# q and k laid out by the host: PE transposes out of a decay attention kernel with a gated projection behind it

## Chip, core and metric

The kernel runs on one core of a Trainium2 chip. The metric is device time in microseconds for one launch; what the host does to the inputs before the launch is not in it. The engines are named as in the profile: PE (TensorE, matrix products), with PEld for its weight loads, DVE (VectorE), ACT (ScalarE), POOL (GpSimd) and SP (SyncE, which issues most DMAs).

## What is computed

Causal attention with a per-position decay for 8 batches of 8 heads (sequence 576, head dimension 64), and on its output a gate from a causal convolution of 5 taps, a 512 x 512 projection, and a second projection.

```python
def _attn_ref(q, k, v, f):
    scores = scale * np.matmul(q, k.transpose(0, 1, 3, 2))
    cum = np.cumsum(np.log(np.clip(f, 0.0001, 1.0)), axis=-1)
    decay = cum[:, :, :, None] - cum[:, :, None, :]
    scores = np.where(causal, -1000000000.0, scores + decay)
    attn = np.exp(scores - np.max(scores, axis=-1, keepdims=True))
    attn = attn / (np.sum(attn, axis=-1, keepdims=True) + 1e-09)
    return np.matmul(attn, v)

def _moe_ref(x, w_val, conv_w, w_out):      # x: heads side by side, (8, 576, 512)
    for k in range(K):                      # K = 5, xp: x padded by 4 in front
        gate_pre += conv_w[k][None, None, :] * xp[:, k:k + S, :]
    gate = 1.0 / (1.0 + np.exp(-gate_pre))
    return gate * (x @ w_val) @ w_out
```

## The kernel before

**Pairs.** Two heads make a pair, and 32 pairs are worked through one after the other; four of them make a batch. A pair's 576 positions are four blocks of 128 rows and a tail of 64. Every product that feeds PE in its fast mode is split into a high part (rounded to the fast type) and a low part (the rest), so that three fast products replace one exact one: for q and k these are the tiles Xh and Xl, for the attention output xh and xl, for the gated value hh and hl. The first four pairs (i < NF) use exact products instead, from one unsplit tile Xf.

**Stages of a pair**, each written by a function of its own:

- `load_pair` (L401) loads q and k of the pair with positions on the partitions: two DMAs of q, two of k, and three small ones for the last 64 rows of both, into qn, kn and zn. `load_rest` (L415) loads the decay rows (dm, dl) and v, three DMAs for v, and masks dm on POOL (L434) and dl (L437).
- `plan_t` (L508) turns q and k on PE, so that the head dimension lies on the partitions: four transposes of q, four of k (L530), two of zn (L537). The result lies in PSUM. For i < NF it is copied to Xf; later DVE or ACT casts it to Xh, and DVE takes the difference to PSUM as Xl (L521).
- `plan_s` (L544) makes the scores, adds the decay and finds the row minimum on DVE (L604), takes the exponential on ACT (L608), and the normalisation (L380, L382) on POOL, DVE or ACT.
- `plan_pt` (L636) turns the probabilities on PE (L649, L667) and copies them out of PSUM into pt; `plan_pv` (L682) multiplies by v, copies the result to x, splits it into xh and xl (L718 on POOL) and makes the gate's convolution: for the first four pairs on PE, with diagonal matrices, later as five passes on DVE (L747; the first tap through L380 or L382).
- After the fourth pair of a batch `plan_moe` (L754) takes the sigmoid on ACT, multiplies by w_val on PE, gates and splits on DVE, ACT and POOL, and multiplies by w_out.

The weights arrive in a packed form and are decoded on ACT and DVE (`plan_w`, `decode`), conv_w too (`plan_cw`), which is also turned on PE (L871).

**What sets the order.** No instruction is issued where it is written. Each is handed to a planner (`Plan.add`, `Plan.dma`) with the engines that may run it, a duration for each, and a priority. `Plan.order` then goes through a modelled time and takes at each step the instruction that can start first, by priority among those that can start together, and so fixes one engine and one place on it for everything. Two tables steer it: OFF moves the priority of a class of instructions, PEN burdens a class on one of its engines, both by stage of the program. PORT names the classes of DVE instructions that the planner keeps apart from POOL's, and STICK how much PE prefers its present array mode. SP's queue and the engines are in order: what stands first is waited for.

Of the kernel before, what the change touches and what calls it, by code (L numbers as in the profile page):

```python
# [32 lines left out]
XZ, XK4, XK, XW = 512, 640, 704, 1216  # L33

# [9 lines left out]
OFF = {  # L44
# [21 lines left out]
}  # L66
PEN = {
# [5 lines left out]
    ("conv", "ACT"): (0.0, 0.0, 2.52, 7.5, 4.7, 2.58), ("conv", "DVE"): (0.0, 0.0, 0.38, 0.0, 0.0, 0.5),  # L73
    ("conv", "POOL"): (0.0, 0.0, 65.48, 22.89, 42.2, 42.68), ("cut0", "DVE"): (12.46, 0.0, 0.0, 0.0, 0.0, 0.0),
    ("diag", "DVE"): (0.33, 1.54, 0.91, 0.0, 0.0, 0.0), ("diag", "POOL"): (11.96, 28.56, 14.33, 0.0, 0.0, 0.0),
    ("hh", "ACT"): (0.0, 0.0, 0.06, 0.0, 0.0, 7.62), ("hh", "DVE"): (0.0, 0.0, 0.22, 12.6, 5.06, 1.54),
    ("hl", "DVE"): (0.0, 0.0, 9.17, 0.64, 3.65, 0.0), ("hl", "POOL"): (0.0, 0.0, 0.51, 0.54, 0.04, 22.01),
    ("load", "ACT"): (7.36, 0.0, 0.0, 0.0, 0.0, 0.0), ("load", "SP"): (0.03, 0.0, 0.0, 0.0, 0.0, 0.0),
    ("norm", "ACT"): (0.0, 0.04, 0.67, 0.05, 0.79, 15.64), ("norm", "DVE"): (0.77, 5.49, 22.53, 0.36, 6.39, 2.21),
    ("norm", "POOL"): (3.05, 17.25, 0.28, 44.42, 0.8, 0.08), ("sel", "DVE"): (29.3, 28.29, 53.65, 8.66, 76.26, 0.31),  # L80
    ("sel", "POOL"): (1.34, 0.0, 0.11, 0.0, 0.0, 9.64), ("start", "ACT"): (5.02, 0.0, 0.0, 0.0, 0.0, 0.0),
    ("start", "DVE"): (5.62, 0.0, 0.0, 0.0, 0.0, 0.0), ("start", "POOL"): (0.21, 0.0, 0.0, 0.0, 0.0, 0.0),
# [197 lines left out]
def tile_decay_attention_gated_mlp(  # L280
    ctx: ExitStack,
    tc: tile.TileContext,
    q: bass.AP,
    k: bass.AP,
# [8 lines left out]
    B, H = q.shape[0], q.shape[1]  # L293
# [3 lines left out]
    KC = conv_w.shape[0]  # L297
# [103 lines left out]
    def load_pair(i):  # L401
        b, h0 = divmod(i, G)
        h0, r = 2 * h0, i % NQ
        p = i - (1.0 if i else 9.0)
        for nm, src, t in (("qn", q, qn[r]), ("kn", k, kn[r])):
            for h in range(2):
                load("load", 0.6, p, t[:, :, h], src[b, h0 + h, 0:L0].rearrange("(n p) d -> p n d", p=P), (), [(nm, r, h)], early=i == 0)
            if nm == "qn":
                for h in range(2):
                    load("load", 0.1, p, zn[r][D * h:D * h + D, 0, D * h:D * h + D], q[b, h0 + h, L0:], [("zn0", r)], [("zq", r, h)], early=i == 0)  # L410
            else:
                load("load", 0.15, p, zn[r][0:D, 1].rearrange("p (h d) -> p h d", h=2), k[b, h0:h0 + 2, L0:].rearrange("h p d -> p h d"),
                     [("zn0", r)], [("zk", r)], early=i == 0)

    def load_rest(i):  # L415
        b, h0 = divmod(i, G)
        h0, r = 2 * h0, i % NQ
# [34 lines left out]
    for r in range(NQ):  # L452
        dve("start", 0.2, z + r, lambda r=r: nc.vector.memset(zn[r], 0.0), (), [("zn0", r)])
# [54 lines left out]
    def plan_t(i):  # L508
        r = i % NQ
        p = float(i) if i else -8.0  # L510

        def evict(nm, key, lo, n, pr):
            if i < NF:
                any_("TF", ap(n), pr, lambda eng: copy(eng, Xf[:, lo:lo + n], bank(key)[:, 0:n]), [key, *kxf], [("Xf", nm)])
                return

            def hi(eng):
                copy(eng, Xh[r][:, lo:lo + n], bank(key)[:, 0:n])

            def low():  # L520
                nc.vector.tensor_tensor(out=Xl[r][:, lo:lo + n], in0=bank(key)[:, 0:n], in1=Xh[r][:, lo:lo + n].bitcast(F32),  # L521
                                        op=ALU.subtract)
            any_("TH", ap(n), pr, hi, [key], [("Xh", r, nm)])
            dve("TL", n / 960.0 + 0.08, pr, low, [key, ("Xh", r, nm)], [("Xl", r, nm)])
# [416 lines left out]
```

## Time and profile before

| | |
|---|---|
| runs | 590.12, 590.6 and, disturbed, 1100.04 us; median 590.6 |
| profiled execution | span 588.0 us from first to last instruction (its own run time is not listed; the runs' median stands 2.6 us above) |
| granted PE clock | 0.997 on average |
| DMA | 92.54 MB in 136222 packets, 118474 of all under 512 bytes |

How to read it: busy time and share for each engine come first, then the chain that ended last, followed backwards from the last instruction to what released each step. A group's row gives the line, the engine, the operation, the tiles (out<-in), the count, the busy time and the mean of one instruction in ns, and behind the second bar the idle time of the engine just before and who ended it. A timeline row gives start, length, engine and instruction. Two rows on the DMA side belong to the change:

```profile
q1 hardware_dynamic: 136222, 92.54, 57.2%
...
kn<-in_k_dram SPq DMA_DIRECT2D x64, 128.0 KB, 6.3
```

The first is the queue's packets, megabytes and share of the 16 DMA engines' time; the second is an issue group with its count, size and median time to landing.

### The profile page before, as it was taken

The page shows a single profiled execution, that of the slowest core. Times are in us where ns is not written, and L with a number is a line of the kernel's source. Part 1 is how long each engine was busy: PE and PEld are TensorE (multiplying, and loading weights), DVE is VectorE, ACT ScalarE, POOL GpSimd, SP SyncE. Part 2 cuts the span into 40 slices and gives each one's busy share as a digit, 9 for nine tenths or more (in the row PEclk, how much of TensorE's full clock was granted, in tenths as well). Part 3 has the DMA queues.
Part 4 walks back from the last instruction along what each step waited for, and adds up shares of the span by engine and source line. Part 5 has one row for each costly group of instructions (what it writes and reads, how often), then busy time and mean ns, then how long its engine had stood idle before and what let it go on. Part 6 is the DMA issues. An engine that isn't in the chain of part 4 may idle for free.

```text
span 588.0 us, 14152 instructions
## 1 busy us (share of the span) xinstructions
PE 566.3 (96%) x4773; PEld 493.8 (84%) x4773; DVE 449.9 (77%) x1200; ACT 460.9 (78%) x1252; POOL 251.6 (43%) x397
## 2 busy tenths in 40 slices
PE   6798989999999999999999999999999999999997
PEld 5576768888789988889888998989988998889995
DVE  5668969799987989779778888696767778775550
ACT  4979969999987698779898889987887786984201
POOL 5121257333322654553554654343664666371200
PEclk9999999999999999999999999999999999999999
DMA  5999787575754566385667666564666645210002
GB/s 136 258 223 262 167 232 220 155 180 158 232 134 137 147 186 192 116 236 145 174 160 194 173 178 178 166 179 124 171 200 171 169 131 163 81 47 19 37 37 89
DMA packets 136294, 93.44 MB, mean 159 GB/s; under 512 B 118474, under 2 KB 118494, under 8 KB 136222
## 3 DMA queue, kind: packets, MB, share of 16 engines
q1 hardware_dynamic: 136222, 92.54, 57.2%
q8 instruction: 38, 0.62, 0.5%
q14 instruction: 34, 0.28, 0.2%
HBM read 82.60 MB, written 9.91 MB: 157 GB/s over the span
## 4 chain that ended last, share of the span: by engine, by line
PE 70%; DVE 10%; ACT 7%; DMA 7%; issue 2%; SPq 2%; POOL 1%; DVEq 0%; POOLq 0%; ACTq 0%
PE banks L360 56%; PE banks L649 8%; DVE banks L604 4%; ACT P L608 3%; PE banks L530 3%; SPq L387 2%; DVE gate L747 2%; DMA vt<-in_v_dram 2%; PE banks L667 1%; DMA ot<-in_moe_w_out_dram 1%; ACT pt L375 1%; DMA dm<-decd 1%; DMA ot<-in_moe_w_val_dram 1%; DMA wu<-in_moe_w_val_dram 1%; DVE negm L604 1%
## 5 line engine op out<-in xcount | busy, mean ns | idle before, releaser
L608 ACT ACTIVATE P<-banks,negm 128x128 f32<-128x128 f32 (+3 forms) x256 | 132.9, 536 | 26.6 <-DVE negm L604 26.3
L604 DVE CUSTOM_DVE_ANT_0 banks<-banks,dm 128x128 f32<-128x128 f32 (+3 forms) x256 | 120.6, 515 | 30.3 <-PE banks L360 19.1
L375 ACT COPY pt<-banks 128x256 f32<-128x256 f32 (+2 forms) x320 | 115.9, 437 | 28.7 <-PE banks L649 24.2
L382 POOL TENSOR_SCALAR P<-P,rz 128x384 f32<-128x384 f32 (+3 forms) x134 | 79.7, 611 | 73.3 <-DVE rz L618 36.7
L360 PE MATMUL banks<-xh,wall 128*128 128x288 f32 x512 | 108.7, 299 | 1.5 <-ACT pt L375 1.4
L747 DVE SCALAR_TENSOR_TENSOR gate<-x,cw,gate 128x576 f32<-128x576 f32 x112 | 103.0, 920 | 1.8
L360 PE MATMUL banks<-pt,vt 128*64 128x128 f32 (+2 forms) x1408 | 97.0, 293 | 3.5 <-ACT pt L375 2.9
L360 PEld LDWEIGHTS banks<-pt,vt 128*64 128x64 f32 x1408 | 86.0, 138 | 15.6 <-ACT pt L375 4.3
L434 POOL TENSOR_SCALAR_AFFINE_SELECT dm<-dm 128x256 f32<-128x256 f32 x126 | 55.7, 467 | 96.6 <-DMA dm<-decd 90.2
L360 PE MATMUL banks<-wall,hh 128*128 128x512 f32 x288 | 93.0, 404 | 1.1 <-ACT P L608 0.9
L649 PE MATMUL banks<-ident,P 128*128 128x128 f32 x640 | 89.3, 277 | 4.0 <-ACT P L380 1.4
L360 PEld LDWEIGHTS banks<-xh,wall 128*128 128x128 f32 x512 | 83.5, 188 | 3.6 <-ACT pt L375 1.6
L649 PEld LDWEIGHTS banks<-ident,P 128*128 128x128 f32 x640 | 71.3, 140 | 12.2 <-ACT P L380 3.4
L360 PE MATMUL banks<-xl,wall 128*128 128x288 f32 x256 | 75.4, 295 | 0.0
L718 POOL TENSOR_TENSOR xl<-x,xh 128x576 fp32r<-128x576 f32 x32 | 50.6, 1583 | 48.9 <-ACT xh L375 48.9
L360 PEld LDWEIGHTS banks<-wall,hh 128*128 128x128 f32 x288 | 51.0, 188 | 11.7 <-ACT P L608 2.3
L360 PE MATMUL banks<-Xh 128*128 128x288 f32 (+4 forms) x280 | 58.4, 346 | 0.6 <-ACT P L608 0.5
L380 ACT ACTIVATE P<-P,rz 128x128 f32<-128x128 f32 (+3 forms) x114 | 58.2, 574 | 0.6 <-DVE rz L618 0.3
L360 PE MATMUL banks<-wall,hl 128*128 128x512 f32 x144 | 56.5, 392 | 0.0
L608 ACT ACTIVATION_READ_ACCUMULATOR P<-banks,negm 128x1 f32 x256 | 54.1, 211 | 0.0
L360 PE MATMUL banks<-Xh,Xl 128*128 128x288 f32 (+4 forms) x280 | 52.9, 314 | 0.0
L360 PE MATMUL banks<-Xl,Xh 128*128 128x288 f32 (+4 forms) x280 | 52.9, 313 | 0.0
(108 smaller groups left out, 933.3 us busy)
## 6 DMA issues: line engine op xcount, KB each, us to landing
dm<-decd SPq DMA_DIRECT2D x62, 640.0 KB, 5.9
out_dram<-ot SPq DMA_DIRECT2D x36, 256.0 KB, 2.3
dl<-decd SPq DMA_DIRECT2D x62, 144.0 KB, 3.7
qn<-in_q_dram SPq DMA_DIRECT2D x64, 128.0 KB, 2.8
kn<-in_k_dram SPq DMA_DIRECT2D x64, 128.0 KB, 6.3
vt<-in_v_dram SPq DMA_DIRECT2D x64, 128.0 KB, 3.1
zn<-in_q_dram SPq DMA_DIRECT2D x64, 16.0 KB, 3.1
zn<-in_k_dram SPq DMA_DIRECT2D x32, 32.0 KB, 2.8
```

Of the source, the lines that this page charges most:

```text
L360: nc.tensor.matmul(out, lhsT=lhsT, rhs=rhs, start=start, stop=stop)
L375: (eng.copy if eng is nc.scalar else eng.tensor_copy)(out=out, in_=in_)
L380: eng.activation(out=out, in_=in_, func=AF.Copy, scale=col)
L382: eng.tensor_scalar(out=out, in0=in_, scalar1=col, scalar2=0.0, op0=ALU.mult, op1=ALU.add)
L387: lambda e: (nc.sync if e == "SP" else nc.scalar).dma_start(out=out, in_=in_), reads, writes, **kw)
L434: nc.gpsimd.affine_select(out=t, in_=t, pattern=[[0, 2], [-1, P]], base=0, channel_multiplier=1, compare_op=ALU.is_ge, fill=-BIG)
L530: nc.tensor.transpose(out=bank(key)[:, n * P:(n + 1) * P], in_=src[:, n].rearrange("p h d -> p (h d)"), identity=ident)
L604: nc.vector.tensor_tensor_reduce(out=sl, in0=sl, in1=add[:, o:o + ext], op0=ALU.add, op1=ALU.min, scale=-0.125, scalar=3.0e38, accum_out=n ...
L608: nc.scalar.activation(out=dst[:, o:o + ext], in_=bank(key)[:, c0:c0 + ext], func=AF.Exp, bias=negm[r][:, col], scale=-1.0, accum_out=zs[r ...
L649: nc.tensor.transpose(out=bank(key)[:, c:c + P], in_=Pt[m][:, BOFF[b] + P * j:BOFF[b] + P * j + P], identity=ident)
L718: any_("xl", {"POOL": 1.4, "DVE": 0.67}, p, lambda eng: eng.tensor_tensor(out=xl[s], in0=xv, in1=xh[s][:, :].bitcast(F32), op=ALU.subtract ...
L747: eng.scalar_tensor_tensor(out=gt, in0=src, scalar=wt_, in1=gt, op0=ALU.mult, op1=ALU.add)
```

## The change

The host now lays the inputs out. q and k of a pair come as one array x of 128 rows (head and head dimension) by 1216 columns, already turned: q's first 512 positions, the two tails of q on a block diagonal, k's tail, k's first 512. v comes padded to five blocks, so that one DMA fills vt with the zeros in it, and conv_w comes turned. Nothing but transposing, padding and packing is done there.

```diff
 XZ, XK4, XK, XW = 512, 640, 704, 1216
+XP = ((0, XK4), (XK4, XW))
...
-    qn = tiles(NQ, [P, NB, 2, D], F32, "qn")
-    kn = tiles(NQ, [P, NB, 2, D], F32, "kn")
-    zn = tiles(NQ, [P, 2, P], F32, "zn")
+    Xr = tiles(NQ, [P, XW], F32, "Xr")
...
     def load_pair(i):
-        for nm, src, t in (("qn", q, qn[r]), ("kn", k, kn[r])):
...
+        r = i % NQ
+        load("load", 1.55, i - (1.0 if i else 9.0), Xr[r], x[i], (), [("Xr", r)], early=i == 0)
...
-        for h in range(2):
-            load("load", 0.6, p + 0.4, vt[r][:, 0:NB, h], v[b, h0 + h, 0:L0].rearrange("(n p) d -> p n d", p=P), [("vt0", r)], [("vt", r, h)])
+        load("load", 0.85, p + 0.4, vt[r], v[i], (), [("vt", r)])
...
     def plan_t(i):
+        if i < NF:
+            return
...
+        for n, (a, e) in enumerate(XP):
+            def hi(eng, a=a, e=e):
+                copy(eng, Xh[r][:, a:e], Xr[r][:, a:e])
+            def low(eng, a=a, e=e):
+                eng.tensor_tensor(out=Xl[r][:, a:e], in0=Xr[r][:, a:e], in1=Xh[r][:, a:e].bitcast(F32), op=ALU.subtract)
+            c = e - a
+            any_("TH", {"ACT": c / 1200.0 + 0.09, "DVE": c / 1920.0 + 0.09, "POOL": c / 1450.0 + 0.4}, i + 0.02 * n, hi, [("Xr", r)], [("Xh", r, n)])
+            any_("TL", {"DVE": c / 960.0 + 0.085, "POOL": c / 415.0 + 0.2}, i + 0.02 * n, low, [("Xr", r), ("Xh", r, n)], [("Xl", r, n)])
-                nc.tensor.transpose(out=bank(key)[:, n * P:(n + 1) * P], in_=src[:, n].rearrange("p h d -> p (h d)"), identity=ident)
...
-        more, opd = 1.0, (lambda *nms: [(x, r, nm) for x in ("Xh", "Xl") for nm in nms])
+        more, opd = 1.0, [(x, r, n) for x in ("Xh", "Xl") for n in range(len(XP))]
         if i < NF:
-            prods, more, opd = ((Xf, Xf),), 4 / 3, lambda *nms: [*(("Xf", nm) for nm in nms), *kxf]
+            prods, more, opd = ((Xr[r], Xr[r]),), 4 / 3, [("Xr", r)]
...
-STICK = 24.84
+STICK = 73.6
-PORT = {"norm", "conv", "hh", "hl", "xl", "xh", "sel", "wv", "wo", "cw", "start", "st0", "cut0", "cuth", "cutl"}
+PORT = {"TH", "TL", "norm", "conv", "hh", "hl", "xl", "xh", "sel", "wv", "wo", "cw", "start", "st0", "cut0", "cuth", "cutl"}
...
```

So the ten PE transposes of a pair go, and with them their PSUM banks and evictions. From pair 4 on Xh is a cast from SBUF to SBUF in two pieces of 640 and 576 columns, by ACT, DVE or POOL, and Xl a subtraction of two SBUF tiles in the same pieces, by DVE or POOL. The scores wait for both pieces of Xh and of Xl; the tail's scores and the main ones waited for their own pieces before. In `plan_cw` the transpose and its eviction go. All of OFF and PEN has new numbers, so the planner gives another order and other engines everywhere.

The three places that follow show what this does to the order. On PE, around the scores of pair 25 (the seventh batch's second pair; Xh, Xl, qn and kn as above, P the probabilities to be turned, banks PSUM), before:

```order
L360 MATMUL banks<-Xh_80 128x512 x2
L360 MATMUL banks<-Xh_80,Xl_82 128x512 x2
L360 MATMUL banks<-Xl_82,Xh_80 128x512 x2
L360 MATMUL banks<-Xh_80 128x256 x2
L360 MATMUL banks<-Xh_80,Xl_82 128x256 x2
L360 MATMUL banks<-Xl_82,Xh_80 128x256 x2
L530 MATMUL banks<-ident,qn_74 128x128 x4
L530 MATMUL banks<-ident,kn_76 128x128 x4
L649 MATMUL banks<-ident,P_84 128x128 x6
L360 MATMUL banks<-wall,hh_117 128x512 x2
```

Here eight transposes for a later pair stood between the scores and the next probabilities. The same scores on PE after the change:

```order
L605 MATMUL banks<-ident,P_79 128x128 x2
L351 MATMUL banks<-Xh_76 128x512 x2
L351 MATMUL banks<-Xh_76,Xl_78 128x512 x2
L351 MATMUL banks<-Xl_78,Xh_76 128x512 x2
L351 MATMUL banks<-Xh_76 128x256 x2
L351 MATMUL banks<-Xh_76,Xl_78 128x256 x2
L351 MATMUL banks<-Xl_78,Xh_76 128x256 x2
L351 MATMUL banks<-pt_85,vt_88 64x128
```

The product with v now follows the scores directly, and no transpose of q or k stands anywhere on PE. On POOL, in the middle of the program (the normalisation L382, the masks of the decay rows L434 and L437, the low split of the attention output L718), before:

```order
L382 TENSOR_SCALAR P_84<-P_84,rz_98 128x384
L382 TENSOR_SCALAR P_84<-P_84,rz_98 128x128
L382 TENSOR_SCALAR Pl_87<-Pl_87,rz_98 128x576
L437 TENSOR_TENSOR dl_71<-dl_71,tri 128x64
L382 TENSOR_SCALAR P_85<-P_85,rz_97 128x384
L382 TENSOR_SCALAR P_83<-P_83,rz_97 128x384
L718 TENSOR_TENSOR xl_109<-x_99,xh_103 128x576
L434 AFFINE_SELECT dm_70<-dm_70 128x2x128 x2
```

On POOL after the change (L366 is the cast to Xh, L492 the subtraction to Xl, L373 the normalisation, L412 and L415 the masks):

```order
L373 TENSOR_SCALAR Pl_82<-Pl_82,rz_93 128x576
L366 CAST Xh_76<-Xr_74 128x640
L366 CAST Xh_76<-Xr_74 128x576
L415 TENSOR_TENSOR dl_72<-dl_72,tri 128x64
L492 TENSOR_TENSOR Xl_78<-Xr_74,Xh_76 128x640
L412 AFFINE_SELECT dm_70<-dm_70 128x2x128 x2
L412 AFFINE_SELECT dm_68<-dm_68 128x2x128 x2
L366 CAST Xh_75<-Xr_73 128x640
L366 CAST Xh_75<-Xr_73 128x576
L492 TENSOR_TENSOR Xl_77<-Xr_73,Xh_75 128x640
L492 TENSOR_TENSOR Xl_77<-Xr_73,Xh_75 128x576
```

POOL gives most normalisations and 19 of 32 subtractions to xl away and takes 38 of the 56 casts to Xh and 41 of the 56 subtractions to Xl. On SP, from the program's start, before (u is the packed conv_w, decd the decay table in DRAM, ot and wu take packed weights):

```order
L387 DMA Pl_87<-in_f_dram 64x576 x2
L387 DMA u_115<-in_moe_conv_w_dram 20x256
L387 DMA qn_73<-in_q_dram 128x4x64 x2
L387 DMA zn_77<-in_q_dram 64x64 x2
L387 DMA kn_75<-in_k_dram 128x4x64 x2
L387 DMA zn_77<-in_k_dram 64x2x64
L387 DMA vt_91<-in_v_dram 128x4x64 x2
```

On SP from the start after the change:

```order
L378 DMA u_111<-in_conv_w_dram 128x40
L378 DMA vt_87<-in_v_dram 128x640
L378 DMA Xr_74<-in_x_dram 128x1216
L378 DMA vt_88<-in_v_dram 128x640
L378 DMA ot<-in_w_val_dram 128x1024
L378 DMA wu<-in_w_val_dram 128x1024
L378 DMA Xr_73<-in_x_dram 128x1216
L378 DMA decd<-gate_109 16x1856
```

Two weight loads and pair 1's x (Xr_74) now stand ahead of pair 0's x (Xr_73), and f is loaded from ACT's queue, behind ACT's table load. In the counts of the order, evictions of pt go from 320 on ACT to 180 on ACT and 140 on DVE, x from 64 on ACT to 36 and 28, ot from 36 on ACT to 26 and 10; normalisations go from 127 on ACT, 11 on DVE and 150 on POOL to 191, 50 and 47; the first conv tap goes from 28 on DVE to 17 on ACT, 8 on DVE and 3 on POOL; SP issues 237 DMAs where it issued 495.

More of the change, by code (lines that the diff above doesn't have):

```diff
@@ L66 @@
 }
 PEN = {
[5 rows of a table removed]
[L73 to L82, printed above, removed]
[5 rows of a table removed]
[6 rows of a table added]
@@ new lines @@
+    ("conv", "ACT"): (0.0, 0.0, 1.53, 0.452, 0.1644, 0.3648), ("conv", "DVE"): (0.0, 0.0, 0.0, 0.0, 0.4151, 0.02559),
+    ("conv", "POOL"): (0.0, 0.0, 0.0, 0.3164, 0.8502, 2.579), ("diag", "DVE"): (1.298, 0.0, 0.0, 0.0, 0.0, 0.0),
+    ("hh", "ACT"): (0.0, 0.0, 0.9759, 0.0, 0.2268, 0.0), ("hh", "DVE"): (0.0, 0.0, 0.0, 2.235, 0.8069, 0.0),
+    ("hl", "DVE"): (0.0, 0.0, 0.0, 0.0, 0.9559, 0.6277), ("hl", "POOL"): (0.0, 0.0, 0.0, 0.1505, 0.0, 1.492),
+    ("load", "ACT"): (0.525, 0.0, 0.0, 0.0, 0.0, 0.0), ("load", "SP"): (0.5314, 0.0, 0.0, 0.0, 0.0, 0.0),
@@ L88 @@
+    ("norm", "ACT"): (0.0, 0.2404, 0.4967, 0.0, 0.3814, 0.4591), ("norm", "DVE"): (0.0, 0.7375, 0.0, 1.087, 0.2988, 0.0),
+    ("norm", "POOL"): (0.1011, 0.3132, 0.0, 1.976, 0.6308, 0.1922), ("sel", "DVE"): (0.0, 0.1277, 0.355, 0.8174, 0.108, 0.6918),
+    ("sel", "POOL"): (0.0, 0.0, 0.02743, 0.1805, 0.408, 1.328), ("start", "DVE"): (0.2423, 0.0, 0.0, 0.0, 0.0, 0.0),
+    ("start", "POOL"): (0.1981, 0.0, 0.0, 0.0, 0.0, 0.0), ("start", "SP"): (0.5586, 0.0, 0.0, 0.0, 0.0, 0.0),
[5 rows of a table added]
 }
@@ L296, in tile_decay_attention_gated_mlp @@
     DM = H * D
-    KC = conv_w.shape[0]
+    KC = conv_w.shape[1] // G
     R = B * H
@@ L343, in tile_decay_attention_gated_mlp @@
     g1 = gate[1].rearrange("p g s -> p (g s)")
-    Xf, wz, wh = g1[:, 0:XW], g1[:, XW:XW + DM], g1[:, XW + DM:XW + 2 * DM]
+    wz, wh = g1[:, XW:XW + DM], g1[:, XW + DM:XW + 2 * DM]
     wm = wh.bitcast(I32)
-    kxf = [("gate", 1, n) for n in range(3)]
     kz, kh, kg = [("wz",)], [("wh",)], [("gate", 1, n) for n in (2, 3)]
     ebias = const.tile([P, 1], F32, name="ebias")
-    cwu = u32.bitcast(I32)[0:KC * G, 0:2 * P]
+    cwu = u32.bitcast(I32)[:, 0:2 * KC * G]
     NBANK = 8
@@ L588, in plan_s @@
             two = 1 + bool(tab)
-            pe("S", (1.15, 0.88, 0.8)[u] * more * two, p, go, (opd("q", "k") if u < 2 else opd("z", "k")) + tab,
+            pe("S", (1.15, 0.88, 0.8)[u] * more * two, p, go, opd + tab,
                list(dict.fromkeys(keys.values())), cols=(2304, 1536, 1728)[u] * more * two, mode=0 if u == 2 else 1)
@@ L687, in plan_pv @@
         xr = x32[r]
-        vk = [("vt0", r), *(("vt", r, n) for n in range(3))]
+        vk = [("vt", r)]
         for half, (qa, qb) in enumerate(((0, 384), (384, 576))):
@@ L862, in plan_cw @@
         NW = KC * G
-        cm, cz, ch = (x[0:NW, 0:P] for x in (wm, wz, wh))
+        cm, cz, ch = (t[:, 0:NW] for t in (wm, wz, wh))
         p = 0.3
         kl = [("cwl",)]
-        load("cw", 0.06, p, cwu, conv_w.bitcast(I32).rearrange("k (g p) -> (k g) p", g=G), (), [("cwu",), *kl])
+        load("cw", 0.1, p, cwu, conv_w.bitcast(I32), (), [("cwu",), *kl])
         cy = decode("cw", p, cwu, cm, cz, ch, [("cwu",)], kl)
-        dve("cw", 0.2, p, lambda: nc.vector.tensor_tensor(out=cz, in0=cz, in1=cy, op=ALU.mult), kz + kl + kg, kz)
-        dve("cw", 0.2, p, lambda: nc.vector.tensor_tensor(out=ch, in0=ch, in1=cz, op=ALU.add), kh + kz + kg, kh)
-        key = new(("cw", 0))
-        pe("cw", 0.1, p, lambda: nc.tensor.transpose(out=bank(key)[:, 0:NW], in_=ch, identity=ident[0:NW, 0:NW]), [*kh, *kg, ("ident",)], [key],
-           mode=0)
-        dve("cw", 0.1, p, lambda: nc.vector.tensor_copy(out=cw.rearrange("p k g -> p (k g)"), in_=bank(key)[:, 0:NW]), [key], [("cw",)])
+        dve("cw", 0.1, p, lambda: nc.vector.tensor_tensor(out=cz, in0=cz, in1=cy, op=ALU.mult), kz + kl + kg, kz)
+        dve("cw", 0.1, p, lambda: nc.vector.tensor_tensor(out=cw.rearrange("p k g -> p (k g)"), in0=ch, in1=cz, op=ALU.add),
+            kh + kz + kg, [("cw",)])
     def plan_w(nm, src, hi_, lo_, p0):
@@ L912, in tile_decay_attention_gated_mlp, with laid_out @@
             last[e] = ins
-_INS = ['q', 'k', 'v', 'f', 'moe_w_val', 'moe_conv_w', 'moe_w_out']
 _OUTS = [((8, 576, 512), 'float32')]
+def laid_out(q, k, v, f, moe_w_val, moe_conv_w, moe_w_out):
+    import numpy as np
+    B, H, _, _ = q.shape
+    G = H // 2
+    qt, kt = (a.reshape(B * G, 2, S, D).transpose(0, 1, 3, 2) for a in (q, k))
+    x = np.zeros((B * G, 2, D, XW), q.dtype)
+    x[..., 0:L0] = qt[..., 0:L0]
+    for h in range(2):
+        x[:, h, :, XZ + D * h:XZ + D * h + D] = qt[:, h, :, L0:]
+    x[..., XK4:XK] = kt[..., L0:]
+    x[..., XK:] = kt[..., 0:L0]
+    vp = np.zeros((B * G, 2, (NB + 1) * P, D), v.dtype)
+    vp[:, :, 0:S] = v.reshape(B * G, 2, S, D)
+    vp = vp.reshape(B * G, 2, NB + 1, P, D).transpose(0, 3, 2, 1, 4)
+    cw = moe_conv_w.reshape(-1, G, P).transpose(2, 0, 1).reshape(P, -1)
+    return {"x": x.reshape(B * G, P, XW), "v": vp, "f": f, "w_val": moe_w_val, "conv_w": cw, "w_out": moe_w_out}
 def kernel(**inputs):
@@ L927 @@
     arrays, args = {}, []
-    for name in _INS:
-        a = _np.ascontiguousarray(inputs[name])
+    for name, a in laid_out(**inputs).items():
+        a = _np.ascontiguousarray(a)
         if a.dtype == _np.float64:
```

59 lines of the change are left out of this document (11 added, 48 removed), and 45 rows, old and new, of tables (OFF, PEN).

## Prediction

> **What bounds the kernel now.** I read the page's busy line first, then the chain that ended last, then the busy time by stage.
>
> ```profile
> span 588.0 us, 14152 instructions
> PE 566.3 (96%) x4773; PEld 493.8 (84%) x4773; DVE 449.9 (77%) x1200; ACT 460.9 (78%) x1252; POOL 251.6 (43%) x397
> ...
> PE 70%; DVE 10%; ACT 7%; DMA 7%; issue 2%; SPq 2%; POOL 1%; DVEq 0%; POOLq 0%; ACTq 0%
> ```
>
> TensorE (PE) is busy 96% of the span and holds 70% of the chain. The median of the runs shown (590.6) is 2.6 us above this span, so I work in the span and add 2.6 at the end. The stages say where PE still waits:
>
> ```profile
> 0.00:100.00 100.00, 87.44 (x637) 67.19 (x638) 74.89 (x221) 79.53 (x224) 37.20 (x79) 0.98 0.81 210
> 100.00:150.00 50.00, 47.67 (x438) 42.47 (x437) 45.40 (x123) 48.59 (x130) 18.47 (x27) 1.00 0.66 183
> 100.00:540.00 440.00, 434.59 (x3862) 387.35 (x3861) 357.35 (x943) 372.86 (x1016) 211.08 (x317) 1.00 0.57 159
> 250.00:300.00 50.00, 49.67 (x442) 44.57 (x442) 41.48 (x109) 43.12 (x126) 26.09 (x36) 1.00 0.70 181
> 540.00:588.00 48.00, 44.27 (x278) 39.24 (x276) 17.66 (x36) 8.48 (x15) 3.35 (x2) 1.00 0.15 55
> ```
>
> The columns are length, then PE, its weight loads, VectorE (DVE), ScalarE (ACT) and GpSimd (POOL) busy, then the granted clock. PE is idle 12.6 us in the first 100, 5.4 in the next 440 and 3.7 at the end: 21.7 in all. From 100 on whatever leaves PE shortens the span one for one, as long as DVE and ACT keep up; they stand at 83% and 86% in a quiet stage (250 to 300). The last 48 us are the projections of the last batches, almost on PE alone; the change does not touch them.
>
> **The transposes that go.** 320 PE transposes (L530, L537) leave.
>
> ```profile
> L530 PE MATMUL banks<-ident,qn 128*128 128x128 f32 x128 | 20.6, 283 | 0.4
> L530 PE MATMUL banks<-ident,kn 128*128 128x128 f32 x128 | 19.5, 275 | 0.1
> L537 PE MATMUL banks<-ident,zn 128*128 128x128 f32 x64 | 12.8, 276 | 0.8 <-DMA zn<-in_k_dram 0.6
> ...
> 401.57 0.38 PE L537 MATMUL banks<-ident,zn 128*128 128x128 f32 x2
> 401.88 0.44 PE L360 MATMUL banks<-Xh 64*128 64x384 f32 x2
> ...
> 411.47 0.66 PE L530 MATMUL banks<-ident,qn 128*128 128x128 f32 x4
> 411.96 0.60 PE L530 MATMUL banks<-ident,kn 128*128 128x128 f32 x4
> 412.40 0.82 PE L649 MATMUL banks<-ident,P 128*128 128x128 f32 x6
> ```
>
> The groups' busy time sums to 52.9 us, but matmuls overlap, so what a group costs PE is the distance to the next start: 0.49 for four of q (411.47 to 411.96), 0.44 for four of k, 0.31 for the two of the tail. That is 1.24 us a pair, 39.7 us for 32. Bounds: 35.2 at the undisturbed step of 0.11 (0.44 for four), 52.9 at the full busy time. I take 39.7, since it is the step itself. The Trainium skill (TensorE: Matmul & The Clock Gate, Part 4: PE-mode transpose) gives about 275 ns for such a transpose inside a kernel; by that figure an estimated 88 us would go and the span would be near 500. The trace has that same 275 as one instruction's duration but starts the next after 110 to 155, so the page's figure is a latency and not a price here.
>
> **Evictions and splits: what moves to DVE, ACT and POOL.**
>
> ```profile
> L375 DVE CAST Xh<-banks 128x512 fp32r<-128x512 f32 x56 | 37.7, 674 | 0.0
> L375 DVE CAST Xh<-banks 128x192 fp32r<-128x192 f32 x28 | 9.8, 350 | 0.3 <-PE banks L537 0.3
> L521 DVE TENSOR_TENSOR Xl<-banks,Xh 128x512 fp32r<-128x512 f32 (+1 forms) x84 | 48.5, 577 | 2.4
> L382 DVE TENSOR_SCALAR gate<-x,cw 128x576 f32<-128x576 f32 x28 | 15.1, 540 | 24.0 <-ACT x L375 23.8
> L382 DVE TENSOR_SCALAR P<-P,rz 128x384 f32<-128x384 f32 x2 | 0.8, 414 | 0.0
> L375 DVE CAST hh<-h 128x576 fp32r<-128x576 f32 x6 | 3.5, 587 | 0.9 <-PE banks L360 0.8
> L805 DVE TENSOR_TENSOR hl<-h,hh 128x576 fp32r<-128x576 f32 x4 | 3.0, 758 | 0.2
> L375 ACT COPY pt<-banks 128x256 f32<-128x256 f32 (+2 forms) x320 | 115.9, 437 | 28.7 <-PE banks L649 24.2 <-PE banks L667 3.8
> L382 POOL TENSOR_SCALAR P<-P,rz 128x384 f32<-128x384 f32 (+3 forms) x134 | 79.7, 611 | 73.3 <-DVE rz L618 36.7 <-ACT P L608 20.3 <-ACT pt L375 9.0
> L382 POOL TENSOR_SCALAR Pl<-Pl,rz 128x576 f32<-128x576 f32 x16 | 12.6, 787 | 0.0
> L718 POOL TENSOR_TENSOR xl<-x,xh 128x576 fp32r<-128x576 f32 x32 | 50.6, 1583 | 48.9 <-ACT xh L375 48.9
> L380 ACT ACTIVATE P<-P,rz 128x128 f32<-128x128 f32 (+3 forms) x114 | 58.2, 574 | 0.6 <-DVE rz L618 0.3
> ```
>
> DVE loses all 84 Xh casts and 84 Xl subtractions from PSUM (96.0), 9 evictions of the first pairs (6 of 512 wide at 0.674 and 3 of 192 at 0.350: 5.1) and 20 first conv taps (10.8): 112. It gains 140 of the 320 pt evictions, 28 of x and 10 of ot (all from PSUM, between 0.22 and 0.67 by width from the 192 and 512 rows: 84), 39 norms at 0.414 (16), 11 Xh casts and 9 xh casts at 0.587 (12), 15 Xl and 19 xl subtractions at 0.758 (26); the rest (weights, diagonals) comes to about -4. Net +22: 449.9 becomes 472. ACT loses 140 pt at 0.437 (61), 28 x, 10 ot and 9 xh (at some 0.5: 24), gains 57 norms at 0.574 and 7 wide ones at 0.787 (38), 7 Xh casts and 17 conv taps (at 0.787 too: 19): about -28, to 433. POOL loses 103 norms (93 at 0.611, 10 at 0.787: 65) and 19 xl (30), gains 38 Xh casts at 0.787 (30), 41 Xl at 1.583 (65) and small change (+6): 258. So nobody but PE comes near its end in total. The total hides a tight stage, though: before the last 48 us DVE is busy 449.9 - 17.7 = 432 of 540 (80%) now, and 472 - 17.7 = 454 of some 503 (90%) then. The stage 100 to 150 above had DVE at 91% and ACT at 97%, and PE was idle 2.33 in 50 (4.7%); the stage 250 to 300, with 83% and 86%, lost 0.33 (0.7%). For the middle 400 us that bounds PE's idle between 2.8 and 18.8. I take 10, between the two because ACT falls while DVE rises: 5 more than now.
>
> **Loads, start, small things.** SP issues 237 DMAs instead of 495; a pair's q and k come in one DMA of 128 rows. In the middle this costs and brings nothing: PE's waits ahead of these transposes are 0.4 + 0.1 + 0.8 us in all, and the cover is a pair's whole period of some 17 us (540 / 32). If that cover failed, the late load would show as PE idle on Xr, at about the landing time of the similar dm load, 5.9 us. At the start it matters more, since SP and the weights are on the chain:
>
> ```profile
> 0.80 1.28 ACT L307 ACT_TABLE_LOAD   x1 [0.80 <-PEq L926]
> ...
> 12.63 1.80 SPq L387
> ...
> 18.77 6.46 DMA ot<-in_moe_w_val_dram
> ...
> 40.29 5.94 DMA wu<-in_moe_w_val_dram
> ...
> 71.98 7.63 DMA ot<-in_moe_w_out_dram
> ...
> dm<-decd SPq DMA_DIRECT2D x62, 640.0 KB, 5.9
> ```
>
> These are 20 us of chain against 12.6 of PE idle, so at most some of the 12.6 can go. The new order issues two weight loads before the table leaves, but pair 0's Xr only as SP's seventh load, and moves the load of f behind ACT's table load. Between -6 (half of the idle) and +2 (f issued 1.3 us later, after the table load, and the wait for Xr) I take -2. The conv_w transpose goes (one PE instruction); memsets of zn and vt go, all beside other work.
>
> Sum: 588.0 - 39.7 (transposes) + 5 (middle) - 2 (start) = 551.3 span, 553.9 as a run: 6% below 590.6.
>
> **Rivals.** (A) *DVE and POOL block each other.* The low split moves from PSUM to two SBUF operands, and such instructions show a lock:
>
> ```profile
> L747 DVE SCALAR_TENSOR_TENSOR gate<-x,cw,gate x112: 776/818/2061, 124.9 to 554.6; 128x576 f32<-128x576 f32 x112
> L718 POOL TENSOR_TENSOR xl<-x,xh x32: 1403/1430/2017, 34.5 to 551.1; 128x576 fp32r<-128x576 f32 x32
> L521 DVE TENSOR_TENSOR Xl<-banks,Xh x84: 350/690/693, 57.5 to 498.3; 128x512 fp32r<-128x512 f32 x56, 128x192 fp32r<-128x192 f32 x28
> ```
>
> With PSUM among its inputs (L521) the maximum equals the median; with SBUF alone (L747) it runs from 0.78 to 2.06 us, the excess being about one POOL instruction. If DVE's SBUF instructions and POOL's long splits collide so that DVE holds 55 us more, DVE needs 472 + 55 plus 42 of its own idle at the two ends (30 of the last 48, and 12, about half of the 25 that it idles in the first 100): 569, as a run 572. It decides once those waits exceed about 37 us (472 + 37 + 42 = 551). Against it: L747's whole excess now is 103.0 - 112 x 0.818, some 11 us. The Trainium skill (SBUF — State Buffer, Who interferes with whom) states this rule: DVE with two SBUF inputs, or in a two-port mode, shuts GpSimd out for a whole instruction and the reverse; the trace agrees by the rows above. By it the splits speak against this change.
>
> (B) *No gain: the transposes filled holes.* PE's idle grows by what goes, and the time stays at 590 (down to 579 if a quarter of it shows). For it: L530 itself is 3% of the chain. Against: 5.4 us of idle in 440.
>
> (C) *Slower: Xl comes late.* On POOL the splits stand behind selections that wait for their DMA:
>
> ```profile
> POOL dm L434 <- DMA dm<-decd: 90.2, 40, 14.2
> ...
> PE banks L360 <- DVE Xl L521: 0.2, 1, 0.2
> ```
>
> Scores now wait for both halves of Xh and Xl. If PE stood 2 us before each of 28 split pairs, 56 come back: 588.0 - 39.7 + 56 + 2.6 = 607. It decides from 39.7 / 28 = 1.4 us a pair. Against: now PE waits 0.2 us for Xl in all, and PE's order has projections to put between.
>
> **How the numbers follow.** The forecast (PE stays the bound, 541 to 562) has 0.68, A (562 to 579) 0.20, B (579 to 602) 0.08, C 0.04. The low end 541 is the lower bound of the start (-6) and the middle (5.4 to 2.8): 588.0 - 39.7 - 6 - 2.6 + 2.6 = 542, and 1 of the way to 52.9. The high end is A at 572 and one more, 573; outside stay C, B and the rest of A, below 0.2. Faster by over 2% (about what a measurement of this kernel can tell from no change), under 578.8: 0.88; within: 0.08; slower: 0.04.
>
> **What would show it.** PE busy near 527 and its idle near 25, with 7 to 12 in the middle: right. L703 (the conv taps) with a mean well over 0.92 and DVE over 500 busy: A. PE busy at 527 with idle over 55: B if the idle is spread, C if its releaser is Xl. A start idle over 15 would make the start term wrong.

## The result, and the profile after

The changed kernel takes 595.2 us in the median of 20 runs, against 590.4 for the kernel before: a ratio of 1.008, with a 95% interval of 1.0061 to 1.01. The forecast was 553.9. Nothing was gained: the time stays the same within 1%, slightly above. The later runs, in the next section, give 563.4 us for the same data path in another order.

The first lines of the profile after hold the busy time and count of each engine, and the shares of the chain that ended last; below them stand granted clock and busy time by stage, for the kernel before and then the one after.

```profile
span 592.6 us, 12921 instructions
PE 548.4 (93%) x4452; PEld 470.0 (79%) x4452; DVE 472.0 (80%) x1266; ACT 444.2 (75%) x1152; POOL 265.9 (45%) x358
...
PE 57%; DVE 19%; ACT 12%; DMA 6%; issue 4%; POOL 1%; SPq 1%; POOLq 0%; DVEq 0%; ACTq 0%
...
L703 DVE SCALAR_TENSOR_TENSOR gate<-x,cw,gate 128x576 f32<-128x576 f32 x112 | 99.5, 891 | 5.2 <-ACT gate L371 4.1
```

```profile
core 0: 588.0 us, clock 0.997
0.00:100.00 100.00, 87.44 (x637) 67.19 (x638) 74.89 (x221) 79.53 (x224) 37.20 (x79) 0.98 0.81 210
100.00:500.00 400.00, 394.59 (x3503) 351.55 (x3503) 329.19 (x870) 341.03 (x935) 193.94 (x293) 1.00 0.61 170
```

```profile
core 0: 592.6 us, clock 0.971
0.00:100.00 100.00, 86.80 (x558) 65.55 (x559) 75.23 (x208) 76.21 (x203) 47.82 (x81) 0.90 0.66 219
100.00:200.00 100.00, 87.74 (x748) 76.15 (x747) 80.96 (x221) 77.67 (x200) 50.31 (x59) 0.95 0.53 165
100.00:500.00 400.00, 375.20 (x3289) 328.61 (x3288) 344.85 (x941) 337.77 (x879) 208.22 (x269) 0.98 0.56 173
```

The reader is to see three things. The 321 PE instructions are gone, and DVE holds the 472 us of the sum. PE is idle 24.8 us in the stretch from 100 to 500 (400 - 375.2), where it was idle 5.4. And the clock fell from 0.997 to 0.971. The span times the missing share of the clock is 17.2 us, against 1.8; the slow clock can have cost at most that, since PE is idle in some of the slow time.

The worst part is 100 to 200, where PE idles 12.3 us while DVE is busy 81% and ACT 78%. No engine is full there; engines wait for each other. PE's largest waits in 100 to 500 (us in total, times, longest) are short and many:

```profile
PE banks L605 <- ACT P L371: 5.7, 4, 3.1
PE banks L351 <- DVE pt L366: 3.9, 6, 1.1
PE banks L351 <- ACT P L564: 3.6, 5, 1.2
PE banks L605 <- ACT x L366: 3.1, 4, 1.5
PE banks L605 <- DVE P L373: 2.5, 1, 2.5
```

The longest of them in the timeline (start, length, engine, instruction, and in brackets the idle time before), followed by the windows around it (length, PE, PEld, DVE, ACT, POOL busy, granted clock):

```profile
173.78 0.29 PE L351 MATMUL banks<-Xl,Xh 128*128 128x288 f32 x1
177.19 0.97 PE L605 MATMUL banks<-ident,P 128*128 128x128 f32 x4 [3.11 <-ACT P L371]
...
175.49 0.77 ACT L564 ACTIVATE Pl<-banks,negm 128x576 f32<-128x576 f32 x1
176.41 3.73 ACT L371 ACTIVATE P<-P,rz 128x512 f32<-128x512 f32 x8
```

```profile
170.60:174.00 3.40, 2.94 (x27) 2.37 (x23) 3.33 (x17) 3.40 (x11) 2.92 (x5) 1.00 0.56 207
174.00:177.40 3.40, 0.29 (x3) 0.21 (x3) 3.33 (x13) 3.33 (x12) 1.92 (x3) 1.00 0.97 294
177.40:180.80 3.40, 3.40 (x30) 3.07 (x30) 3.30 (x5) 3.40 (x8) 1.40 (x4) 0.50 1.00 264
180.80:184.20 3.40, 3.40 (x40) 2.84 (x36) 2.58 (x7) 3.17 (x4) 2.20 (x4) 1.00 0.52 146
```

PE has given out all scores of a pair and the next instruction in its order is the transpose of that pair's P. ACT must first finish the exponentials and then normalise, so PE stands for 3.1 us with nothing else in front. Behind the hole comes a stretch of 3.4 us in which PE works at half speed: the idle time is paid for once more.

### The profile page after: what moved, and what is told of

It is laid out like the page before. It is cut to its first block, busy times and chain, and to the rows that moved or that the text cites. A ratio compares the mean times of both kernels' runs of the same rounds, so it can differ in the third digit from the quotient of the medians.

```text
span 592.6 us, 12921 instructions
## 1 busy us (share of the span) xinstructions
PE 548.4 (93%) x4452; PEld 470.0 (79%) x4452; DVE 472.0 (80%) x1266; ACT 444.2 (75%) x1152; POOL 265.9 (45%) x358
## 4 chain that ended last, share of the span: by engine, by line
PE 57%; DVE 19%; ACT 12%; DMA 6%; issue 4%; POOL 1%; SPq 1%; POOLq 0%; DVEq 0%; ACTq 0%
PE banks L351 47%; PE banks L605 8%; DVE banks L560 6%; DMA dl<-decd 5%; ACT P L564 4%; DVE gate L703 3%; DVE pt L366 2%; ACT P L371 2%; PE banks L623 2%; DVE negm L560 1%; DMA Xr<-in_x_dram 1%; ACT pt L366 1%; DVE rz L573 1%; DVE P L373 1%; ACT gate L719 1%
## 5 line engine op out<-in xcount | busy, mean ns | idle before, releaser
L351 PE MATMUL banks<-xh,wall 128*128 128x288 f32 x512 | 113.6, 307 | 5.3 <-DVE h L748 2.2
L605 PE MATMUL banks<-ident,P 128*128 128x128 f32 x640 | 96.2, 284 | 17.8 <-ACT P L371 6.8
L412 POOL TENSOR_SCALAR_AFFINE_SELECT dm<-dm 128x256 f32<-128x256 f32 x126 | 64.7, 538 | 88.6 <-DMA dm<-decd 67.7
L703 DVE SCALAR_TENSOR_TENSOR gate<-x,cw,gate 128x576 f32<-128x576 f32 x112 | 99.5, 891 | 5.2 <-ACT gate L371 4.1
L351 PE MATMUL banks<-pt,vt 128*64 128x128 f32 (+2 forms) x1408 | 100.8, 296 | 2.9 <-DVE pt L366 1.7
L366 ACT COPY pt<-banks 128x256 f32<-128x256 f32 (+2 forms) x180 | 71.2, 442 | 41.5 <-PE banks L605 36.0
L351 PEld LDWEIGHTS banks<-xh,wall 128*128 128x128 f32 x512 | 86.7, 194 | 8.6 <-DVE h L748 2.4
L371 ACT ACTIVATE P<-P,rz 128x256 f32<-128x256 f32 (+3 forms) x171 | 84.5, 558 | 6.8 <-DVE rz L574 6.2
L492 POOL TENSOR_TENSOR Xl<-Xr,Xh 128x640 fp32r<-128x640 f32 (+1 forms) x41 | 62.9, 1543 | 9.1 <-ACT Xh L366 5.1
L366 DVE COPY pt<-banks 128x512 f32<-128x512 f32 (+2 forms) x140 | 59.6, 461 | 7.7 <-PE banks L605 6.4
```

Source lines behind the costliest of these rows:

```text
L351: nc.tensor.matmul(out, lhsT=lhsT, rhs=rhs, start=start, stop=stop)
L366: (eng.copy if eng is nc.scalar else eng.tensor_copy)(out=out, in_=in_)
L371: eng.activation(out=out, in_=in_, func=AF.Copy, scale=col)
L412: nc.gpsimd.affine_select(out=t, in_=t, pattern=[[0, 2], [-1, P]], base=0, channel_multiplier=1, compare_op=ALU.is_ge, fill=-BIG)
L492: eng.tensor_tensor(out=Xl[r][:, a:e], in0=Xr[r][:, a:e], in1=Xh[r][:, a:e].bitcast(F32), op=ALU.subtract)
L605: nc.tensor.transpose(out=bank(key)[:, c:c + P], in_=Pt[m][:, BOFF[b] + P * j:BOFF[b] + P * j + P], identity=ident)
```

## The experiments

Two theories were to be told apart. **O**: the data path saves PE time as worked out, and the new order (what stands where on which engine) gives it back. **D**: the path itself costs what it saves, by the one large late load, by splits between two SBUF operands, or because the transposes kept PE's clock up. All kernels here compute the whole function.

### The path alone, with the old order held (e1)

Each engine gets the instructions of the kernel before, in their old sequence and old PSUM banks, minus the transposes and their evictions. The casts to Xh and the subtractions to Xl stand where the evictions stood, all of them on DVE.

```diff
-    for fn, e in plan.order(BEGIN):
-        if fn is not None:
-            fn(e)
+    for k, at0 in zip(plan.width, HOMES):
+        plan.home[k] = [int(at0) + n for n in range(plan.width[k])]
+    for step in ORDER:
+        plan.nodes[int(step[1:])]["fn"](NAMES[step[0]])
```

> The new data path alone, with the order held as in the kernel before: every engine gets its remaining instructions in the old sequence and on the old engine, the Q and K transposes and their evictions are dropped, the one Xr load of a pair stands where the first q load of that pair stood, and the casts and subtractions of Xh and Xl stand where the old evictions of q and k stood, on the same engines. Theory O (the path itself saves about 40 us of PE, the new order gives it back in PE idle and in a slower clock): 550 to 572 us, PE busy 525 to 535, PE idle 25 to 45, granted clock 0.98 or more. Theory D (the path costs what it saves, by the late large load, by splits between two SBUF operands, or by transposes missing as work that keeps the clock up): 585 us or more, whatever the order; with PE waits on Xr, Xh or Xl of 20 us or more, or a clock of 0.97 or less.

Measured: 592.4 us, ratio 1.0002 [0.9968, 1.0037]. O's time is refuted, and PE is busy 543.9 us and idle 48.5 where O had 525 to 535 and 25 to 45. The time is one that D names, but D's waits are not there, and the clock of 0.979 lies between O's 0.98 and D's 0.97. The first row below is its 100 to 500, the next two are PE's largest waits over the whole span, the last is POOL's normalisation.

```profile
100.00:500.00 400.00, 373.42 (x3239) 324.80 (x3239) 331.24 (x830) 339.38 (x936) 218.88 (x288) 1.00 0.53 171
...
PE banks L717 <- ACT P L483: 6.8, 6, 1.9
PE banks L717 <- POOL P L485: 6.8, 4, 5.7
...
L485 POOL TENSOR_SCALAR P<-P,rz 128x384 f32<-128x384 f32 (+3 forms) x134 | 97.2, 740 | 74.6 <-DVE rz L686 43.4
```

PE's idle in 100 to 500 is 26.6 us; its largest waits are for P, and none is for Xr, Xh or Xl. I read this as an order that fitted the old work and doesn't fit the new: PE reaches each P sooner, and P isn't there sooner. One thing that D names may have a part in it: POOL's 134 normalisations, the same in number and shape as before, take 740 ns instead of 611, while DVE's 56 Xl subtractions now read two SBUF operands and its 56 casts to Xh read SBUF instead of PSUM. What that cost was not tried by itself.

### The same kernel with other numbers in the tables (e2), and with the old ones (e3)

The numbers of OFF, PEN and STICK were chosen anew for the changed work: small random changes, each kept if the planner's own end came earlier. On record are the numbers that came of it, not the search. The diff has three of the many lines; no operation, load or shape differs.

```diff
-STICK = 73.6
+STICK = 69.378
...
-    "PT": (49.62, 56.57, 267.4, 346.4, -7.965, -87.59), "PV": (-94.93, 139.6, 366.3, 7.853, -26.78, 158.0),
+    "PT": (67.776, -99.58, 0.0, 358.64, -18.15, -87.59), "PV": (0.0, 139.6, 366.3, 7.853, -26.78, 158),
...
-    ("norm", "POOL"): (0.1011, 0.3132, 0.0, 1.976, 0.6308, 0.1922), ("sel", "DVE"): (0.0, 0.1277, 0.355, 0.8174, 0.108, 0.6918),
+    ("norm", "POOL"): (0.1011, 1.9417, 0.0, 2.4986, 0.6308, 0.1922), ("sel", "DVE"): (0.0, 0.61914, 0.355, 0.8174, 0.108, 0.6918),
```

> The changed kernel with other numbers in the three tables that set the order (OFF, PEN, STICK), chosen anew for the changed work; no operation, load or shape differs. Theory O: 545 to 565 us, PE busy 522 to 532, PE idle 20 to 30, granted clock 0.985 or more. Theory D: 585 us or more, since all that it blames is still there. Rival clock (the half-speed stretches come from the data path, by missing warm transposes, and not from the idle gaps): PE busy stays at 540 or more and the clock at 0.97, with a time of 570 to 580.

Measured: 565.9 us, ratio 0.9576 [0.9523, 0.963], 0.9 us above O's range; PE busy 535.3, 3 above it.

```profile
core 0: 564.0 us, clock 0.985
100.00:500.00 400.00, 392.32 (x3458) 347.36 (x3456) 358.98 (x981) 344.16 (x885) 192.44 (x252) 1.00 0.57 175
```

From 100 to 500 PE idles 7.7 us and the clock stays at 1.00. D as the whole account and the rival on the clock are refuted: the same transposes are missing, and the same loads and splits are there. Whether the splits cost something within each order stays open. With the numbers of the kernel before in the same kernel:

> The changed kernel with the numbers that the kernel before has in OFF, PEN and STICK. Theory O: these numbers were chosen for other work, so the order is no better than the new one, 590 to 615 us, the loss again as PE idle (45 us or more) spread over the middle, with releasers on ACT and DVE. Theory D: the order matters little, 590 to 600, with the waits at Xr, Xh and Xl. If it runs below 580, the new numbers alone made the loss.

Measured: 595.1 us, ratio 1.0074 [1.0041, 1.0108], PE idle 17.1 us in 100 to 500 and 45.5 in all, with ACT's pt (11.4) and ACT's P (10.7) as the largest waits over the whole span.

```profile
100.00:500.00 400.00, 382.88 (x3311) 334.00 (x3311) 286.59 (x754) 352.09 (x962) 240.44 (x326) 0.99 0.55 173
```

Both theories name this time, so the waits decide: none of PE's is for Xr, Xh or Xl. O was wrong on the place, for it had the idle time spread over the middle, and 28 of the 45.5 us lie outside it. The old numbers are no better than the new ones; neither set suits this work.

### Which numbers (e7, e8), and a control (e9)

```diff
-    "PT": (49.62, 56.57, 267.4, 346.4, -7.965, -87.59),
+    "PT": (49.62, -99.58, 267.4, 346.4, -7.965, -87.59),
```

> The changed kernel with one number of its tables changed: the offset of the transposes of P for pairs 1 and 2 (OFF of PT, second place) from 56.57 to -99.58, which puts the transposes of P of these two pairs earlier in TensorE's order; everything behind is ordered anew from there. Theory O (the loss is the order's, not the path's): 568 to 585, with TensorE's waits in 100 to 200 us, 12.3 us in the changed kernel, under 7. Theory D: 590 or more, since the path is untouched; also if the gain of e2 came from the many other numbers that it changes, 590 or more.

Measured: 580.1 us, ratio 0.9821 [0.9772, 0.9871]: 15 us from one number. PE idles 7.3 us in 100 to 200 instead of 12.3, slightly above the 7 expected. Over the whole middle its idle time falls less, from 24.8 to 20.6 us:

```profile
core 0: 579.1 us, clock 0.982
100.00:500.00 400.00, 379.38 (x3303) 335.61 (x3298) 349.86 (x960) 330.12 (x862) 192.29 (x243) 0.98 0.56 174
```

Of the 13.5 us that the span loses against the changed kernel, 10.6 are PE's busy time (548.4 to 537.8), of these up to 6.8 by the clock. So the first number alone brings more through fewer half-speed stretches than through shorter waits.

```diff
-    ("norm", "POOL"): (0.1011, 0.3132, 0.0,
+    ("norm", "POOL"): (0.1011, 1.942, 0.0,
```

> As e7, and a second number: the price that keeps the normalisations of pairs 1 and 2 off GpSimd (PEN of norm on POOL, second place) from 0.3132 to 1.942, so that they go to ACT and DVE. Theory O: 562 to 572, about what e2 with all its changed numbers gives (565.9). If these two numbers aren't the core of it: 575 or more.

Measured: 563.4 us, ratio 0.9544 [0.9516, 0.9571], the fastest of all. Its lines:

```profile
PE 533.8 (95%) x4452; PEld 461.6 (82%) x4452; DVE 470.9 (84%) x1294; ACT 442.4 (79%) x1148; POOL 247.3 (44%) x334
...
core 0: 561.2 us, clock 0.988
0.00:100.00 100.00, 81.94 (x576) 61.75 (x577) 76.62 (x229) 80.85 (x224) 43.87 (x73) 0.93 0.69 229
100.00:500.00 400.00, 394.38 (x3461) 348.70 (x3461) 356.84 (x981) 344.36 (x885) 194.46 (x253) 1.00 0.55 175
```

DVE, ACT and POOL are loaded as in the changed kernel (471, 442 and 247 us against 472, 444 and 266), yet PE's idle in 100 to 500 is 5.6 us instead of 24.8. POOL's 19 us less is not the reason, for in e7 POOL has 252 us and PE idles 20.6. The load of an engine did not make the waits; the place of its instructions did, which engine holds them included. Both numbers touch pairs 1 and 2 alone, but all later choices follow from the earlier ones, so the order differs from there to the end. The control is the kernel before with newly chosen numbers (in a search at least as long, which judged each order on several slightly disturbed sets of the planner's durations, so not quite in the way of e2):

> Control: the kernel before, with OFF, PEN and STICK chosen anew in the same way as those of e2; the data path is the old one. If a new choice of numbers is worth something by itself, it shows here. Theory O (e2's gain is the path's, once an order fits it): 585 to 592, within 1% of the kernel before. Rival (the gain of e2 is the choice of numbers, and the path brings little): 570 or less.

Measured: 596.6 us, ratio 1.0094 [1.0057, 1.0132]. It lies above O's range: that choice was a little worse than the given one. This one newly chosen order of the old path gains nothing, which speaks against the rival. PE's own work says more: PE is busy 566.3 us in the kernel before and 570.9 here, both at a clock of 0.997, and both lie above e8's whole span of 561.2. An order of the old path without a single wait would still be slower than e8, unless it also shortened PE's busy time. What stays open is whether some other order of the old path would be faster than the given one.

### The price of the transposes (e5, e6), and the clock (e4)

```diff
                     t = bank(keys[0])
+                    for n in range(10):
+                        nc.tensor.transpose(out=t[:, n % NB * P:(n % NB + 1) * P], in_=ident, identity=ident)
                     for a, e in ((0, 288), (288, 576)):
```

> The retuned kernel with ten transposes of the identity put ahead of the last score group of each pair, 320 in all, written into the bank that the scores then overwrite: as many as the change took out, with no eviction and no wait of their own. If TensorE bounds this order, they cost their full step, 320 x 0.124 = 39.7 us: 600 to 608. If transposes fall into holes that exist anyway (the rival of no gain), less than 20: under 586.

> The changed kernel as it was given, with the same 320 transposes at the same places. Theory O (its order leaves TensorE waiting for other engines, and the holes bring the half clock): part of the 39.7 us falls into holes, and the work also keeps the clock up, so the time rises by 10 to 30 us, to 605 to 625. If the order's holes took the whole gain of the change, it rises by under 10. If TensorE bounds it fully, by 38 or more, 633.

Measured: 589.0 us for the retuned kernel with them (ratio 0.999 [0.9969, 1.0011]), 23.1 above e2 and between the two expectations; 612.7 for the changed kernel with them (1.0378 [1.0351, 1.0405]), 17.5 above it and as O has it. In the timeline of the first, ten such transposes and what follows them:

```profile
308.37 1.25 PE L530 MATMUL banks<-ident 128*128 128x128 f32 x10
309.38 0.38 PE L351 MATMUL banks<-Xh 128*128 128x288 f32 x1
```

Ten take 1.01 us to the next start, 32 us for 320, so the step of these transposes was 0.10 and not 0.124. Of these 32, 23 show where PE is mostly the bound, and they undo e2's whole gain; 17.5 show in the order with holes. Some of the rest filled idle time: PE's idle falls from 28.7 to 24.8 us in the first (564.0 - 535.3 against 587.6 - 562.8) and from 44.2 to 37.2 in the second (592.6 - 548.4 against 610.9 - 573.7). Some was repaid by the clock, which rises from 0.985 to 0.988 and from 0.971 to 0.980; by the span that is worth up to 1.4 and 5.0 us. So the rival of no gain was partly true, for 4 to 7 of the 32 us fell into holes.

```diff
-        for n in range(NB):
-            nc.tensor.transpose(out=bank(wk)[:, n * P:(n + 1) * P], in_=ident, identity=ident)
+        for n in range(7):
+            nc.tensor.transpose(out=bank(wk)[:, n % NB * P:(n % NB + 1) * P], in_=ident, identity=ident)
```

> The retuned kernel (e2_retuned) with one edit: each of the six warm-up groups ahead of the first scores does 7 transposes of the identity instead of 4, 18 more in all, so that TensorE works in the hole between 6.0 and 9.5 us in which e2 waited. Theory clock (a stretch of 3.4 us in which TensorE idles some 1.5 us or more is followed by a stretch at half speed): the half-speed stretch that e2 showed from 8.3 to 15.1 us goes, TensorE's busy time falls by 2 to 4 us in the first 30 us though it does more work, and the run falls by 1 to 4 us against e2, to 562 to 565. Rival (the clock at the start is low for another reason, or the start hangs on other engines): the stretch stays, or the time stays within 1 us of e2's 565.9 or rises by the up to 2 us that the added transposes may reach past 9.5 us.

Measured: 565.85 us, ratio 0.9609 [0.9581, 0.9636]; e2 has 565.9 and 0.9576 with an interval that overlaps, so no gain shows, as the rival has it. PE's busy time in the first 30 us did not fall by 2 to 4 us either; it went from 22.4 to 22.8. The windows of e2 stand first, then those of this run:

```profile
4.90:8.30 3.40, 1.05 (x9) 0.81 (x8) 2.00 (x4) 0.68 (x1) 1.23 (x3) 1.00 0.96 328
8.30:15.10 6.80, 5.61 (x18) 3.50 (x20) 2.65 (x9) 3.59 (x7) 2.46 (x4) 0.50 0.84 276
```

```profile
4.90:8.30 3.40, 3.12 (x27) 2.88 (x26) 1.42 (x4) 0.68 (x1) 1.24 (x3) 1.00 0.89 321
8.30:15.10 6.80, 5.27 (x35) 3.85 (x36) 3.40 (x9) 3.60 (x7) 2.46 (x4) 1.00 0.83 283
...
19.18 2.29 PE L351 MATMUL banks<-Xr 128*128 128x288 f32 x4 [2.63 <-ACT P L564]
```

With the hole filled the half-speed stretch is gone, as the theory on the clock says. PE ends its scores sooner, though, and waits 2.63 us for ACT's exponential (last row), and behind that hole the clock is halved from 18.8 on. The sixth pair's last exponential still starts 1.9 us earlier than in e2 (85.0 against 86.9), but later a hole opens that e2 does not have:

```profile
96.84 0.40 PE L351 MATMUL banks<-Xh 128*128 128x288 f32 x1 [2.08 <-ACT P L564]
```

It brings another half-speed stretch, and the last pair's exponential starts 2.5 us later than in e2 (499.7 against 497.2). The two profiled executions took 568.2 and 565.7 us, though, while the medians are equal, so a part of these 2.5 us may be that one execution's. The run shows that a filled hole keeps the clock up there, and not what that is worth. That a gain of 2 us in a fixed order shifts which waits meet later is read from this one trace.

## Why the prediction was wrong

**The step that failed is the middle term**: "For the middle 400 us that bounds PE's idle between 2.8 and 18.8. I take 10". It came to 24.8 in the changed kernel. The bounds were read from two stages of the kernel before by how busy DVE and ACT were, as if idle time followed from load. The two numbers of e8 show that it doesn't: with nearly these loads PE idles 5.6 or 24.8 us, by the order. The changed kernel alone shows it too: DVE is busy 86% and ACT 84% of this stretch, less than in the stage that gave the upper bound (91% and 97%), and yet PE idles more than the bound of 18.8. The diff gave all new numbers of the tables, so an order unlike the old one was known; its waits were taken from the old one.

**The clock has no term at all.** The sum took PE's busy time as 566.3 - 39.7 = 526.6, so at the old clock. The loss by the clock is up to 17.2 us instead of 1.8.

The 41.3 us between the forecast span of 551.3 and the measured 592.6 are thus: 14.4 more idle in the middle (24.8 against 5.4 + 5), 2.6 at the start (13.2 in the first 100 us against 12.6 - 2), 2.5 at the end (44.2 - 13.2 - 24.8 = 6.2 against 3.7), and 21.8 more of PE's busy time, up to 15.4 of it by the clock. The remaining 6.4 or more are not settled.

**What held.** The transposes leave PE, and that shortens the time once the order fits: e8 is 26.8 us below the kernel before in span, 561.2 against 588.0. The sum had 36.7. The difference of 9.9 is the start (5.5 us more idle than before in the first 100, where 2 less were taken: 7.5), the clock (6.7 against 1.8: 4.9), the middle (5.6 where 10.4 stood: -4.8) and 2.3 of busy time that is not settled. "From 100 on whatever leaves PE shortens the span one for one" was too strong: e5 shows 23 of 32. DVE's 472 was met, in part by luck: its norms came to 22 us more than before instead of 16, and the taps (L703) to 3.5 less. ACT came to 444 against 433, POOL to 266 against 258. The load of x costs PE nothing in the middle, as taken: PE waits for Xr 0.5 us in all. Other loads are less clear, for between 100 and 500 the chain that ended last passes through four loads of dl for 23.5 us; what these cost was not tried.

**The rivals.** (A) fell in size: L703 has a mean of 891 ns, below the 920 that was its sign, and DVE's 472 us leave no room for 55 more. Its mechanism does show in places. At 110.44 in the changed kernel DVE's normalisation of 384 columns runs beside POOL's split:

```profile
110.06 3.34 POOL L492 TENSOR_TENSOR Xl<-Xr,Xh 128x640 fp32r<-128x640 f32 x2 [1.94 <-ACT Xh L366]
...
110.44 1.69 DVE L373 TENSOR_SCALAR P<-P,rz 128x384 f32<-128x384 f32 x1
...
112.28 0.86 PE L605 MATMUL banks<-ident,P 128*128 128x128 f32 x4 [2.49 <-DVE P L373]
```

It takes 1.69 us where the kernel before has 0.414, and PE waits 2.49 us for it. The Trainium skill (SBUF — State Buffer, Who interferes with whom) says that DVE with two-port access and GpSimd shut each other out for a whole instruction; this place agrees. That this collision made the wait is read from the trace and was not tried; at 0.414 us the normalisation would have ended 1.3 us sooner, so it accounts for about half of the 2.49 at most. (B), no gain with idle spread over the middle (whose lower value should read 580.7, 590.6 less a quarter of 39.7), is nearest to what happened, though not at the values that were to show it: PE's idle is 44 us where over 55 was named, and its busy time 548 and not 527, with most of the difference in busy time within what the slow clock can have cost. (C) fell: no large wait is for Xl.

## What to carry to other kernels

When a change takes work from the engine that bounds a statically ordered kernel, how much of that work's price is kept depends on the order (here 26.8 of the forecast 39.7 us in the best one, and nothing in the given one), and neither the old order nor the old numbers behind it need fit the new work. Idle time could not be forecast here from how busy the other engines are: of two orders with nearly the same loads, one lost 19 us more. So before a data path is judged by one time, try it in more than one order, with a control that orders the old path anew.

## What was not expected of the hardware

Holes in PE's work much shorter than 3.4 us bring a half-speed stretch of 3.4 or 6.8 us. In the eleven traces the granted clock went from full to half 37 times while work was left, each time behind a stretch of 3.4 us in which PE was idle 1.48 to 3.41 us; no stretch at full speed with more than 1.88 us of idle time was followed by full speed. The idle time is the sum of a stretch, in one or several holes, and between 1.48 and 1.88 us both outcomes occur. One case of each kind near the border, from e2 and from e7:

```profile
18.60:22.00 3.40, 1.92 (x6) 0.59 (x4) 3.33 (x14) 2.95 (x10) 1.56 (x3) 1.00 0.87 287
22.00:25.40 3.40, 2.82 (x12) 2.32 (x12) 2.89 (x10) 3.36 (x10) 0.84 (x1) 0.50 1.02 400
```

```profile
68.40:71.80 3.40, 1.54 (x13) 1.33 (x13) 3.37 (x12) 3.35 (x13) 0.00 (x0) 1.00 0.86 287
71.80:75.20 3.40, 3.40 (x19) 2.82 (x20) 3.35 (x8) 2.55 (x7) 1.93 (x3) 1.00 0.60 225
```

The Trainium skill (TensorE: Matmul & The Clock Gate, Part 1) has the half rate behind an idle window of some 3.4 us; here about half a window of idle time was enough. So by estimate a wait of 2 us can cost PE up to 1.7 us more, half of the 3.4 that follow, or twice that if the slow stretch lasts 6.8 us, where PE is the bound.
